# Attention outputs put into their transposed layout by evictions and 32x32 VectorE transposes instead of TensorE transposes

## The chip, the cores and the metric

The kernel runs on one NeuronCore of a Trainium2 chip. TensorE (PE in the profile) multiplies matrices from SBUF into PSUM, whose eight banks each hold 128 partitions x 512 fp32; ScalarE (ACT) and VectorE (DVE) read PSUM and SBUF, GpSimd (POOL) reads and writes SBUF here, and SyncE (SP) issues the DMAs. Each engine executes its own instruction list in order; semaphores tie the lists together. The metric is the device time of one execution in microseconds (us); the kernel before took 704.47 us in the median of three runs (704.37 to 705.89).

## The reference

A transformer block on x of shape (1, 2048, 448) in fp32, with adaLN conditioning:

```python
mod = (_silu(c) @ w_mod).reshape(c.shape[0], 6, 1, -1)     # sa, ca, ga, sb, cb, gb
h = _layernorm(x) * (1 + ca) + sa
x = x + ga * _A_ref(h, A_wqkv, A_wo)       # attention: 16 heads of 28, causal window of 256
h = _layernorm(x) * (1 + cb) + sb
x = x + gb * _B_ref(h, B_w1, B_b1, B_w2)   # 448 -> 1792, mish, 1792 -> 448
```

Attention: for each head, softmax over the keys j with 0 <= i - j < 256 of q.k / sqrt(28), times v; the heads are put side by side and multiplied with wo.

## The kernel before, in words

**Precision.** Nearly every product is made from fp32 values split into a high part (hi, fp32r) and a remainder (lo): x*w is hi*hi + hi*lo + lo*hi, three matmuls. The contraction over 448 rows takes four chunks ci of 128; the last has only 64 rows, and its two halves are used for hi and lo together, so a product takes 3+3+3+2 = 11 matmuls ("passes" and the list `ps` in `gen_wo`).

**Stages.** The 2048 rows are four groups g of 512. After a start of some 48 us, one loop runs over 192 units u: unit u is a third (k = u mod 3) of one head of one group, a slot s = u // 3 being one head. In step u the program emits, in this order: stages of a small pipe (evictions of earlier filler work), `PV(u-3, Pl)`, the eviction `EV` where a head is complete, scores `B(u)` with two exponentials on ACT (P in fp32, Ph in fp32r), `SP(u-1)` (Pl = P - Ph on POOL), a row-maximum pass `A` for a head three slots ahead (a matmul into sA, then a DVE reduction with the mask), every sixth step `M2` (the maxima of two heads turned by TensorE, split on DVE and sent by DMA into rows of q), then filler, and `PV(u-2, Ph)`. A has four tiles a slot: one in each step and a second one at the end of step k = 1. The filler on PE is the QKV projection of the next group and the wo projection of the group before, paid out by a credit (`RATE` us a step). After the loop comes the feed-forward part (two matmul stages, 56 blocks), in which the wo projection of the last group is still interleaved.

**PSUM.** Eight banks: sA 2, sB 2, mm 2 (filler), pv 1, tr 1 (M2's transpose and the output transposes `et`).

**From the head's sum to the wo product.** `PV` accumulates for one head a 60 x 512 tile: rows 0 to 27 from v hi, row 28 the sum of the probabilities (a column of ones in V), rows 32 to 59 from v lo. `EV` (L748) copies it on ACT into half of o2. For two heads together, `E` (L755) turns it by four TensorE transposes into `et`, `E2` (L762) copies the lo part out on ACT, and `E3` (L766) on DVE takes the reciprocal of the sums and adds hi and lo, and on POOL multiplies into `on`, whose rows are tokens. When a group is complete `gen_oT` (L614) turns `on` back by 16 TensorE transposes (`ot`), because the wo matmuls want features on the partitions; ACT takes the high part from PSUM (L624) and DVE the remainder (L619). `gen_wo` (L637) then makes four tiles of 11 matmuls each (issued at L315). `E` and `E3` are emitted once for two heads, 32 times in all; `gen_oT` runs once a group, for the last group in the feed-forward part.

## Time and profile before

| | value |
|---|---|
| median of three runs | 704.47 us (704.37 to 705.89) |
| the profiled execution: span | 703.9 us |
| its own time beside the span | only the span is recorded for it; it lies 0.6 us under the median of the runs |
| start, before the first unit | 0 to 48 us |
| attention loop | 48 to 412 us |
| feed-forward | 412 to 704 us |
| TensorE clock granted | 1.00 in every stage |

Busy shares are shares of the span. A matmul's "mean ns" is its latency from start to modelled end; matmuls overlap, so what one costs in a stream is the distance to the next start, read from the timeline. "Idle before" gives the time an engine stood still before an instruction of a group, and what released it. PEld is the loading of weights, which runs beside PE.

### The profile page before, as it was taken

What the parts mean: (1) busy time and instruction counts of PE and PEld (TensorE: products, weight loads), DVE (VectorE), ACT (ScalarE), POOL (GpSimd) and SP (SyncE); (2) the same over time, 40 slices, a digit from 0 to 9 for tenths busy, and PEclk for the clock granted to TensorE, in tenths of its full rate; (3) what the DMA queues carried; (4) which work ended last, traced back from release to release, by engine and by line L of the source; (5) the groups of instructions that cost most, each with busy time, mean ns of one, the idle gap of its engine ahead of it and who ended that gap; (6) DMA issues with size and microseconds to landing.
All of it is one profiled execution on the core that took longest, in us unless ns stands there. A gap on an engine that the chain in (4) does not pass through costs nothing.

```text
span 703.9 us, 11999 instructions
## 1 busy us (share of the span) xinstructions
PE 685.9 (97%) x4001; PEld 590.2 (84%) x4001; DVE 383.3 (54%) x1030; ACT 391.6 (56%) x740; POOL 326.4 (46%) x355
## 2 busy tenths in 40 slices
PE   9899999999999999999999899999999999999997
PEld 8777888888888888898887788878888888888886
DVE  5688658788655887655768755452224222421112
ACT  3628788777667867667878974344233323332221
POOL 6626779686666776666778957212010000000000
PEclk9999999999999999999999999999999999999999
DMA  7865664455662462663773165800350035001001
GB/s 209 259 221 188 208 204 152 139 181 157 181 209 76 158 207 88 185 211 95 226 216 120 54 203 170 227 20 1 104 117 4 0 106 119 1 1 52 1 1 52
DMA packets 75178, 90.16 MB, mean 128 GB/s; under 512 B 31535, under 2 KB 51741, under 8 KB 75117
## 3 DMA queue, kind: packets, MB, share of 16 engines
q1 hardware_dynamic: 74652, 89.39, 42.0%
q8 instruction: 32, 0.52, 0.3%
q14 instruction: 30, 0.24, 0.1%
q10 hardware_dynamic: 464, 0.00, 0.0%
HBM read 56.60 MB, written 32.51 MB: 127 GB/s over the span
## 4 chain that ended last, share of the span: by engine, by line
PE 78%; DVE 6%; DMA 6%; ACT 3%; POOL 3%; issue 3%; SPq 1%; DVEq 0%; POOLq 0%; ACTq 0%
PE z L917 17%; PE pv L745 10%; PE qk L315 8%; PE sA L683 5%; PE acc L1106 5%; PE acc L1104 5%; PE acc L1105 5%; PE sB L713 5%; PE wo L315 4%; PE qk_v L315 4%; PE sB L724 3%; DMA scr<-st 2%; PE et L759 2%; PE warm L428 1%; DVE junk L685 1%
## 5 line engine op out<-in xcount | busy, mean ns | idle before, releaser
L735 POOL TENSOR_TENSOR Pl<-P,Ph 128x512 fp32r<-128x512 f32 (+2 forms) x192 | 234.8, 1230 | 80.9 <-ACT Ph L728 46.6
L685 DVE CUSTOM_DVE_ANT_0 junk<-sA,mask 128x384 f32<-128x384 f32 (+2 forms) x256 | 135.1, 528 | 95.1 <-PE sA L683 87.4
L727 ACT ACTIVATE P<-sB 128x512 f32<-128x512 f32 (+2 forms) x192 | 109.6, 571 | 62.3 <-PE sB L724 58.1
L925 DVE TENSOR_TENSOR al<-t,ah 128x512 fp32r<-128x512 f32 x56 | 39.2, 700 | 181.8 <-ACT ah L924 181.8
L923 ACT ACTIVATE t<-z,b1c 128x512 f32<-128x512 f32 x56 | 38.3, 684 | 138.6 <-PE z L917 138.6
L728 ACT ACTIVATE Ph<-sB 128x512 fp32r<-128x512 f32 (+2 forms) x192 | 109.2, 569 | 0.0
L683 PE MATMUL sA<-k,q 84*128 84x384 f32 (+2 forms) x256 | 100.5, 396 | 1.8 <-DVE mx L685 1.1
L917 PE MATMUL z<-hlf,w 128*128 128x512 f32 x224 | 88.6, 395 | 0.0
L917 PE MATMUL z<-hhf,w 128*128 128x512 f32 x224 | 88.6, 395 | 0.0
L1104 PE MATMUL acc<-w2h,ah 128*128 128x448 f32 x224 | 82.2, 367 | 1.2 <-ACT ah L924 1.2
L1106 PE MATMUL acc<-w2h,al 128*128 128x448 f32 x224 | 82.1, 366 | 0.1
L1105 PE MATMUL acc<-w2l,ah 128*128 128x448 f32 x224 | 81.6, 364 | 0.0
L745 PE MATMUL pv<-Ph,v 128*60 128x256 f32 (+2 forms) x352 | 76.7, 292 | 0.6 <-ACT o L751 0.5
L745 PE MATMUL pv<-Pl,v 128*60 128x256 f32 (+2 forms) x352 | 74.0, 284 | 2.4 <-POOL Pl L735 1.4
L713 PE MATMUL sB<-q,k 86*128 86x256 f32 (+1 forms) x352 | 74.2, 285 | 0.5 <-DMA q<-mr 0.5
L917 PE MATMUL z<-hhf,w1l 128*128 128x512 f32 x168 | 66.3, 395 | 0.0
L713 PEld LDWEIGHTS sB<-q,k 86*128 86x128 f32 x352 | 61.5, 189 | 2.3 <-DMA q<-mr 1.5
L724 PE MATMUL sB<-fdmask,identr 128*128 128x128 bf16 (+1 forms) x320 | 60.1, 253 | 0.0
L745 PEld LDWEIGHTS pv<-Ph,v 128*60 128x60 f32 x352 | 45.8, 133 | 14.0 <-ACT o L751 1.9
L745 PEld LDWEIGHTS pv<-Pl,v 128*60 128x60 f32 x352 | 45.2, 132 | 11.5 <-POOL Pl L735 3.8
L683 PEld LDWEIGHTS sA<-k,q 84*128 84x128 f32 x256 | 48.9, 193 | 7.0 <-DVE mx L685 4.3
L917 PEld LDWEIGHTS z<-hlf,w 128*128 128x128 f32 x224 | 42.2, 188 | 10.0
(159 smaller groups left out, 1252.4 us busy)
## 6 DMA issues: line engine op xcount, KB each, us to landing
scr<-st SPq DMA_DIRECT2D x24, 512.0 KB
k<-scr SPq DMA_DIRECT2D x48, 252.0 KB
q<-scr SPq DMA_DIRECT2D x64, 168.0 KB
scr<-st SPq DMA_DIRECT2D x32, 256.0 KB
x<-x1d SPq DMA_DIRECT2D x10, 448.0 KB
xin<-in_A_x_dram SPq DMA_DIRECT2D x8, 448.0 KB
xr<-in_A_x_dram SPq DMA_DIRECT2D x16, 224.0 KB
x1d<-xr SPq DMA_DIRECT2D x16, 224.0 KB
```

The costliest lines, as they stand in the source:

```text
L315: PE.matmul(p, b, a, start=(n == 0), stop=(n == 10))
L683: PE.matmul(p[:, c0:384], q[0:84, t * 128:(t + 1) * 128], k[0:84, t * 128 + c0:t * 128 + 384], start=True, stop=True)
L685: DVE.tensor_tensor_reduce(out=junk[:, c0:384], in0=p[:, c0:384], in1=mask[:, c0:384], scale=1.0, scalar=-3.0e38, op0=ALU.add, op1=ALU.max ...
L713: PE.matmul(p[:, c:c + 128 * (t1 - t0)], k[:, jj * 128:(jj + 1) * 128], q[:, t0 * 128:t1 * 128], start=(n == 0), stop=False, skip_group_ch ...
L727: ACT.activation(P[:, c0:], p[:, c0:], AF.Exp, scale=SCALE)
L728: ACT.activation(Ph[u][:, c0:], p[:, c0:], AF.Exp, scale=SCALE)
L735: eng.tensor_tensor(Pl[u][:, a:b], Pt[u][:, a:b], Ph[u][:, a:b].bitcast(F32), op=ALU.subtract)
L745: PE.matmul(pv[0:60, t0 * 128:t1 * 128], V[j % NV][:, h, :], P[u][:, c:c + 128 * (t1 - t0)], start=(P is Ph and b == 0 and n == 0), stop=F ...
L917: PE.matmul(zb[n], ps[m][1], ps[m][0], start=(m == 0), stop=(m == 10))
L1104: PE.matmul(p, ah[n][:, ts], w2h[f], start=(f == 0), stop=False)
L1105: PE.matmul(p, ah[n][:, ts], w2l[f], start=False, stop=False)
L1106: PE.matmul(p, al[n][:, ts], w2h[f], start=False, stop=(f == NF - 1))
```

## The change

In the kernel after, the sums of a head stay with features on partitions. V has 61 columns: lo first (0 to 27), zeros, hi (32 to 59), and the ones column at 60. `on` is one tile of 128 x 4 x 512: chunk ci holds four heads, head j of the four on partitions 32j to 32j+28 (28 features and the sum of probabilities), cleared once at the start. `EV` copies hi and the sum on ACT straight to these partitions. The lo part is added by DVE from PSUM for heads 0 and 1 of the four (`EVlo`), and for heads 2 and 3 is copied by ACT into `tmp` and added by POOL (`add_lo`). Every fourth head, `inverse` turns the chunk in 32x32 blocks on DVE into `tmp`, takes 16 reciprocals a partition, and turns them back, repeated over 32 columns, into `tmp`; `divide` multiplies `on` by `tmp` on POOL. The split into hi (ACT) and lo (DVE) follows from SBUF. wo is laid out in the same padded manner: 32 rows a head, loaded as four pieces of 28 rows a chunk into cleared tiles. So all four chunks are 128 rows and each wo tile takes 12 matmuls instead of 11. `E`, `E2`, `E3` and `gen_oT` are gone; the bank of `tr` goes to pv (2 banks), and `M2` takes one of the two sA banks.

```diff
-    V = [... .tile([128, H, 60], F32R, name=f"v{j}") for j in range(NV)]
+    V = [... .tile([128, H, 61], F32R, name=f"v{j}") for j in range(NV)]
@@ v_out
-            ACT.activation(v[:, :, 0:28], pv, AF.Copy)
+            ACT.activation(v[:, :, 32:60], pv, AF.Copy)
-            DVE.tensor_tensor(v[:, :, 32:60], pv, v[:, :, 0:28].bitcast(F32), op=ALU.subtract)
+            DVE.tensor_tensor(v[:, :, 0:28], pv, v[:, :, 32:60].bitcast(F32), op=ALU.subtract)
@@ wo
-    wol = [mid.tile([128, D], F32R, name=f"wol_{i}", tag="wo", bufs=7) for i in range(3)]
+    wol = [mid.tile([128, D], F32R, name=f"wol_{i}", tag="wo", bufs=8) for i in range(4)]
+    def wo_rows(ci, t):
+        for j in range(4):
+            r = (4 * ci + j) * DH
+            dma(t[32 * j:32 * j + DH], wo[r:r + DH, :])
+            POOL.memset(t, 0.0)
+            later.append(lambda ci=ci, t=t: wo_rows(ci, t))
+    on = mid.tile([128, 4, 512], F32, name="on")
+    POOL.memset(on, 0.0)
@@ in place of gen_oT
+    def split_o(g, ci, pl, own):
+        if ci == 0:
+            OT[g] = new_T(f"o{g}", pl, own)
+        oh, ol = OT[g]
+        ACT.activation(oh[:, ci], on[:, ci], AF.Copy)
+
+        def low():
+            DVE.tensor_tensor(ol[:, ci], on[:, ci], oh[:, ci].bitcast(F32), op=ALU.subtract)
...
+        pipe.add(1, low)
+
+    def split_ready():
+        if ready and (ready[0][0] == 0 or ready[0][0] - 1 in wo_done) and ready[0][0] < NG - 1:
+            split_o(*ready.pop(0), att, "o")
@@ gen_wo
-            for ci in range(3):
+            for ci in range(4):
                 ps += [(oh[:, ci, ts], wo3[ci]), (oh[:, ci, ts], wol[ci]), (ol[:, ci, ts], wo3[ci])]
-            ps += [(oh[:, 3, ts], wo3[3]), (ol[:, 3, ts], wo3[3])]
@@ M2, PV
-        p = bank("tr", 1, f"mt{pr}")
+        p = bank("sA", 2, f"mt{pr}")
+            pvb[i] = bank("pv", 2, f"pv{i}")
@@ in place of EV, E, E2, E3
     def EV(i):
+        g, h = divmod(i, H)
+        ci, j = divmod(h, 4)
+        q = slice(32 * j, 32 * j + DH + 1)
         if i < NS - 3:
+            ACT.activation(on[q, ci], pvb[i][32:61, :], AF.Copy)
+            if j > 1:
+                ACT.activation(tmp[32 * j:32 * j + 32], pvb[i][0:32, :], AF.Copy)
         else:
+            DVE.tensor_copy(on[q, ci], pvb[i][32:61, :])
+    def EVlo(i):
...
+        if j < 2 or i >= NS - 3:
+            o = on[32 * j:32 * j + DH, ci]
+            DVE.tensor_tensor(o, o, pvb[i][0:DH, :], op=ALU.add)
+    def add_lo(n):
...
+            POOL.tensor_tensor(o, o, tmp[64:128], op=ALU.add)
+    def inverse(n):
+        g, ci = divmod(n, 4)
+        DVE.transpose(tmp, on[:, ci])
+        DVE.reciprocal(inv, tmp.rearrange("p (c r) -> p c r", r=32)[:, :, DH:DH + 1])
+        DVE.transpose(tmp.rearrange("p (c r) -> p c r", r=32), inv.to_broadcast([128, 16, 32]))
+    def divide(n):
+        g, ci = divmod(n, 4)
+        POOL.tensor_tensor(on[:, ci], on[:, ci], tmp, op=ALU.mult)
@@ fill_main
-            yield from gen_oT(g - 1, "mm", 2, att, "o")
+            while pipe.held():
+                yield
             yield from gen_qkv(g + 1, (0, 3, 4, 1) + VT)
@@ the loop
+    def outputs(i, u):
+        EV(i)
+        if i % 4 == 3:
+            for d, f in ((1, add_lo), (2, inverse), (3, divide), (5, done_o)):
+                at(u + d, lambda f=f: f(i // 4))
     for u in range(NU + 9):
...
         pipe.step()
+        for f in due.pop(u, ()):
+            f()
+        split_ready()
         if 0 <= u - 3 < NU:
             PV(u - 3, Pl)
             if (u - 3) % 3 == 2:
-                EV((u - 3) // 3)
+                outputs((u - 3) // 3, u)
...
-            if k == 2 and pr >= 0:
-                E(pr)
-        if s % 2 == 0 and k < 2 and 0 <= (s - 4) // 2 < NS // 2:
-            (E2, E3)[k]((s - 4) // 2)
...
         if k == 1 and a < NS:
             A(a, 2)
+        if 0 <= u - 3 < NU and (u - 3) % 3 == 2:
+            EVlo((u - 3) // 3)
```

How the lists move, at three places in the third group (the row says line, operation, output and inputs, shape, and on which engines it waits). First PE, at the end of a slot in which a pair of heads is complete: sA is the maximum pass, et the output transposes, pv the next head's sums. Before:

```order
L683 MATMUL sA_3_3520<-k_0_142,q_0_377 128x384 [waits DVE_49]
L759 MATMUL et_3523<-ident,o_1_465 128x124 x4
L745 MATMUL pv_3531<-Ph_3446,v_171 60x128 [waits Activation_49]
L745 MATMUL pv_3531<-Ph_3446,v_173 60x384
L745 MATMUL pv_3531<-Pl_3487,v_171 60x128 [waits Pool_49]
```

and now:

```order
L693 MATMUL sA_3_3432<-k_0_142,q_0_377 128x384 [waits DVE_49]
L755 MATMUL pv_3439<-Ph_3354,v_171 61x128
L755 MATMUL pv_3439<-Ph_3354,v_173 61x384
L755 MATMUL pv_3439<-Pl_3398,v_171 61x128 [waits Pool_49]
L755 MATMUL pv_3439<-Pl_3398,v_173 61x384
```

The four transposes between the maximum pass and PV are gone, and PV's first matmul no longer waits for ACT. Second DVE, in a step k = 1 (two maximum tiles, ISA junk,mx). Before, the reciprocal and the addition for two heads stand between them:

```order
L685 ISA junk,mx_3451<-sA_0_3547,mask 128x384 [waits PE_49]
L685 ISA mx_3451 128x1
L220 BN_STATS sta_3558<-xin_2838 128x6
L221 BN_AGGR mva_3430<-sta_3558 128x2 [waits DVE_49]
L685 ISA junk,mx_3451<-sA_1_3581,mask 128x384 [waits PE_49]
L685 ISA mx_3451 128x1
L772 RECIPROCAL rc_3584<-et_3523 128x8 [waits Activation_49]
L773 TENSOR_TENSOR ol_3552<-ol_3552,et_3523 128x224 [waits Pool_49]
L685 ISA junk,mx_3451<-sA_2_3599,mask 128x384 [waits DVE_49,PE_49]
L685 ISA mx_3451 128x1
```

and now, in the corresponding place for four heads:

```order
L695 ISA mx_3359 128x1
L703 CAST mr_3365<-mt_3363 8x128 [waits DMAHW5_49,DMAHW4_49,PE_49]
L704 TENSOR_TENSOR mr_3365<-mt_3363,mr_3365 8x128 [waits DVE_49]
L220 BN_STATS sta_3379<-xin_2620 128x6
L221 BN_AGGR mva_3337<-sta_3379 128x2 [waits DVE_49]
L787 STREAM_TRANSPOSE tmp<-on 128x512 [waits Pool_49]
L788 RECIPROCAL inv<-tmp 128x16 [waits DVE_49]
L789 STREAM_TRANSPOSE tmp<-inv 128x512 [waits DVE_49]
L695 ISA junk,mx_3359<-sA_1_3400,mask 128x384 [waits PE_49]
L695 ISA mx_3359 128x1
L695 ISA junk,mx_3359<-sA_2_3411,mask 128x384 [waits DVE_49,PE_49]
L695 ISA mx_3359 128x1
```

The two transposes and the reciprocal stand behind the maximum pass of tile 0 and M2's two small operations, and ahead of the maximum passes of tiles 1 and 2; the first transpose waits for POOL. Third POOL, where Pl is the remainder of the probabilities. Before:

```order
L735 TENSOR_TENSOR Pl_2640<-P_2605,Ph_2606 128x512 [waits PE_49,Activation_49,Pool_49]
L735 TENSOR_TENSOR Pl_2669<-P_2636,Ph_2637 128x512 [waits PE_49,Activation_49,Pool_49]
L775 TENSOR_TENSOR on_2299<-ol_2647,rc_2674 128x4x56 [waits DVE_49]
L735 TENSOR_TENSOR Pl_2704<-P_2665,Ph_2666 128x512 [waits PE_49,Activation_49,Pool_49]
L735 TENSOR_TENSOR Pl_2728<-P_2700,Ph_2701 128x512 [waits PE_49,Activation_49,Pool_49]
L735 TENSOR_TENSOR Pl_2759<-P_2724,Ph_2725 128x512 [waits PE_49,Activation_49,Pool_49]
L735 TENSOR_TENSOR Pl_2791<-P_2755,Ph_2756 128x512 [waits PE_49,Activation_49,Pool_49]
```

and now:

```order
L745 TENSOR_TENSOR Pl_2641<-P_2610,Ph_2611 128x512 [waits PE_49,Activation_49,Pool_49]
L783 TENSOR_TENSOR on<-on,tmp 64x512 [waits Activation_49,Pool_49]
L745 TENSOR_TENSOR Pl_2665<-P_2637,Ph_2638 128x512 [waits PE_49,Activation_49,Pool_49]
L745 TENSOR_TENSOR Pl_2703<-P_2661,Ph_2662 128x512 [waits PE_49,Activation_49]
L793 TENSOR_TENSOR on<-on,tmp 128x512 [waits DVE_49]
L745 TENSOR_TENSOR Pl_2730<-P_2699,Ph_2700 128x512 [waits PE_49,Activation_49]
L745 TENSOR_TENSOR Pl_2755<-P_2726,Ph_2727 128x512 [waits PE_49,Activation_49,Pool_49]
```

One multiplication for two heads has become an addition and a multiplication for four heads; the multiplication waits for DVE and stands ahead of the next Pl.

101 lines of the change are left out of this document (37 added, 64 removed).

## Prediction, made before the result was known

> **What bounds the kernel now.** I read the busy shares first, then a table by stage, then PE's waits, and for each price the timeline. On the profile's page:
>
> ```profile
> PE 685.9 (97%) x4001; PEld 590.2 (84%) x4001; DVE 383.3 (54%) x1030; ACT 391.6 (56%) x740; POOL 326.4 (46%) x355
> ...
> PE 78%; DVE 6%; DMA 6%; ACT 3%; POOL 3%; issue 3%; SPq 1%; DVEq 0%; POOLq 0%; ACTq 0%
> ```
>
> PE fills the span and holds 78% of the chain that ended last. Busy PE is not proof, since a matmul's end is modelled, but the weight loads that run beside it are at 84% too. By stage (time, length, then busy us of PE, PEld, DVE, ACT, POOL, the granted clock, DMA):
>
> ```profile
> 84.00:103.00 19.00, 19.00 (x127) 15.46 (x125) 10.76 (x43) 14.28 (x33) 13.92 (x15) 1.00 0.73 231
> 103.00:122.00 19.00, 19.00 (x128) 16.04 (x127) 15.44 (x47) 16.27 (x39) 17.44 (x17) 1.00 0.46 148
> 122.00:222.00 100.00, 98.73 (x681) 86.64 (x679) 70.76 (x217) 72.47 (x140) 69.01 (x63) 1.00 0.53 164
> 222.00:322.00 100.00, 98.59 (x677) 86.34 (x675) 70.22 (x215) 72.09 (x139) 69.09 (x64) 1.00 0.51 157
> 322.00:369.00 47.00, 46.40 (x318) 39.60 (x318) 31.22 (x98) 35.87 (x71) 34.90 (x30) 1.00 0.65 193
> 369.00:412.00 43.00, 39.36 (x282) 32.81 (x281) 33.06 (x85) 36.17 (x70) 35.35 (x37) 1.00 0.28 86
> 412.00:704.00 292.00, 287.15 (x1334) 248.65 (x1333) 92.84 (x155) 95.98 (x152) 37.50 (x43) 1.00 0.24 69
> ```
>
> The clock is 1.00 throughout. The rows 122 to 322 are groups 1 and 2: PE 98.7 of 100 us, the others near 70. What is taken from PE there comes off the time. In 103 to 122, the end of group 0, POOL has 17.44 of 19 us; in 369 to 412, the loop's end, PE has only 39.4 of 43 and ACT, POOL and DVE stand at 33 to 36: there nothing is gained by PE alone. What PE waits for, in all:
>
> ```profile
> PE pv L745 <- POOL Pl L735: 1.4, 3, 0.5
> ...
> PE sA L683 <- DVE mx L685: 1.1, 3, 0.4
> ```
>
> Both waits are small now, and both are what the change leans on.
>
> **The change part by part: what PE loses and gets.** A stretch of PE's timeline with a pair's four output transposes, then one with four of a group's back transposes, then wo weight loads in a row:
>
> ```profile
> 195.58 0.51 PEld L759 LDWEIGHTS et<-ident,o 124*128 124x128 f32 x4
> ...
> 196.06 0.24 PEld L745 LDWEIGHTS pv<-Ph,v 128*60 128x60 f32 x2
> ...
> 241.86 0.47 PEld L250 LDWEIGHTS ot<-ident,on 128*128 128x128 f32 x4
> ...
> 242.30 0.24 PEld L745 LDWEIGHTS pv<-Ph,v 128*60 128x60 f32 x2
> ...
> 375.14 0.19 PEld L315 LDWEIGHTS wo<-wo,hlo 128*128 128x128 f32 x1
> ...
> 375.35 0.19 PEld L315 LDWEIGHTS wo<-wo,hho 128*128 128x128 f32 x1
> ```
>
> From load to load, four `et` take 196.06 - 195.58 = 0.48 us and four `ot` 242.30 - 241.86 = 0.44; wo matmuls follow at 375.35 - 375.14 = 0.21. So E's 32 quads give 15.4 us, gen_oT's 16 quads 7.0, and 16 more wo matmuls cost 3.4: 19.0 us off PE. By place: group 0 -3.8 (8 quads of et); groups 1, 2 and 3 each -3.8 - 1.8 + 0.8 = -4.8; feed-forward -1.8 + 0.8 = -0.9, the last group's share. PV's matmuls stream the same columns, only 61 instead of 60 weight columns are loaded; the rows below price that.
>
> **What the other engines get.** The rows of the groups on which I draw (name, shapes, count, busy us, mean ns, then idle before):
>
> ```profile
> L1139 DVE STREAM_TRANSPOSE zt<-z 128x512 f32<-128x512 f32 x12 | 8.4, 704 | 0.0
> L339 DVE TENSOR_TENSOR st<-qk,st 128x512 fp32r<-128x512 f32 x28 | 19.2, 686 | 2.5 <-ACT st L336 2.4
> L619 DVE TENSOR_TENSOR hlo<-ot,hho 128x512 fp32r<-128x512 f32 x16 | 10.9, 685 | 5.7 <-ACT hho L624 5.7
> L773 DVE TENSOR_TENSOR ol<-ol,et 128x224 f32<-128x224 f32 x32 | 10.7, 335 | 0.0
> L772 DVE RECIPROCAL rc<-et 128x8 f32<-128x8 f32 x32 | 6.5, 202 | 1.1 <-ACT ol L764 1.1
> L694 DVE TENSOR_TENSOR mr<-mt,mr 8x128 fp32r<-8x128 f32 x32 | 8.9, 279 | 1.1
> L198 DVE TENSOR_TENSOR wol<-wop,wo 128x448 fp32r<-128x448 f32 x3 | 3.5, 1178 | 0.0
> L198 DVE TENSOR_TENSOR w1l<-w1p,w 128x448 fp32r<-128x448 f32 x5 | 3.0, 616 | 0.0
> L220 DVE BATCH_NORM_STATS2 sta<-xin 128x6 f32<-128x448 f32 x16 | 9.9, 618 | 3.6 <-DMA xin<-in_A_x_dram 3.6
> L241 DVE TENSOR_SCALAR xin<-xin,mva,rsa 128x448 f32<-128x448 f32 x12 | 10.1, 840 | 0.5 <-POOL rsa L235 0.5
> L241 DVE TENSOR_SCALAR xn<-x,mv,rsf 128x448 f32<-128x448 f32 x12 | 5.8, 526 | 1.2 <-POOL rsf L235 1.2
> ...
> L735 POOL TENSOR_TENSOR Pl<-P,Ph 128x512 fp32r<-128x512 f32 x155 | 201.9, 1307 | 73.5 <-ACT Ph L728 40.8 <-PE sA L683 11.4 <-POOL Pl L735 6.4
> L775 POOL TENSOR_TENSOR on<-ol,rc 128x224 f32<-128x224 f32 x32 | 18.3, 573 | 21.7 <-DVE ol L773 9.1 <-ACT Ph L728 8.9 <-PE ot L250 1.5
> L160 POOL MEMSET mask<- 128x384 f32 x1 | 0.4, 422 | 0.1
> ...
> L751 ACT ACTIVATE o<-pv 60x512 f32<-60x512 f32 x61 | 35.9, 589 | 22.7 <-PE pv L745 22.3
> L764 ACT ACTIVATE ol<-et 128x224 f32<-128x224 f32 x32 | 11.7, 366 | 0.0
> ...
> L713 PEld LDWEIGHTS sB<-q,k 86*128 86x128 f32 x352 | 61.5, 189 | 2.3 <-DMA q<-mr 1.5
> L745 PEld LDWEIGHTS pv<-Ph,v 128*60 128x60 f32 x352 | 45.8, 133 | 14.0 <-ACT o L751 1.9 <-issue 0.6
> ```
>
> Weights: 128 columns load in 189 ns, 60 in 133, so a column is 0.8 ns; 704 loads get at most 0.6 us, hidden where a load lies beside a matmul. I take nothing.
>
> DVE, for four heads. Gone are two reciprocals and two additions, 2 x (0.20 + 0.34) = 1.07 us. New: two EVlo, a PSUM and an SBUF operand on 512 columns like L339, 1.37; two transposes and a reciprocal, the `inverse`, 0.70 + 0.20 + 0.70 = 1.6. DVE rises by 1.9 us in about 25, from 71 to 78%. The 0.70 is from the feed-forward, where POOL is idle. Beside a running POOL (the loop) three sorts of DVE work are to be seen: a pass with two SBUF inputs takes 1178 ns instead of 616 (L198), L241's scaling of one input 840 instead of 526, and L220 with one input stays at 618. The transpose has one input and the pace of L220 (512/704 = 448/618 = 0.73 elements a ns; L241 alone makes 448/526 = 0.85), so 0.70 is my value; the bounds are 0.70 and 0.70 + 0.56.
>
> The Trainium skill says the same of the cause: "SBUF — State Buffer", section "Who interferes with whom", has a VectorE instruction with at most one SBUF input outside the two-port modes free of contention with GpSimd, and one with two SBUF inputs contending with GpSimd's reads. By that rule the transposes are free, which the trace cannot show before they run beside POOL, and it speaks against another part of the change: the remainder of the split read PSUM and SBUF, and now reads SBUF twice.
>
> That remainder (L619, 685 ns) is priced by L198: 0.56 us more, 16 times, 9 us of DVE, none of it on a chain that PE waits for directly, since a group's wo is due much later. I take nothing, and keep 0 to 4 us for the range.
>
> What decides is the place of `inverse`. It stands behind M2's two DVE passes (0.55 us with L693's copy) and ahead of the step's two maximum passes. How far PE runs ahead of DVE there:
>
> ```profile
> 193.31 0.42 PE L683 MATMUL sA<-k,q 84*128 84x384 f32 x1
> 193.76 0.56 DVE L685 CUSTOM_DVE_ANT_0 junk<-sA,mask 128x384 f32<-128x384 f32 x1 [1.08 <-PE sA L683]
> ...
> 194.87 0.56 DVE L685 CUSTOM_DVE_ANT_0 junk<-sA,mask 128x384 f32<-128x384 f32 x1 [0.54 <-PE sA L683]
> ...
> 195.47 0.42 PE L683 MATMUL sA<-k,q 84*128 84x384 f32 x1
> ```
>
> The pass of 193.76 has freed its bank at 194.32 and PE takes it again at 195.47: 1.15 us of slack, and DVE stood idle 0.54 us before the next pass. A block of 1.6 us uses up the idle time (0.54) and nearly all the slack (1.06 of 1.15), and costs PE nothing when DVE comes to it early. With M2's 0.55 and another eviction (0.69) still in front it is late by up to 1.2. M2 now also turns up in sA's two banks, which shortens the distance between two uses of a bank. Bounds 0 and 1.2, I take 0.45 us for each of the 15 blocks of the loop, 1.8 a group.
>
> POOL, for four heads: 2 x 0.57 goes, an addition (64 partitions, the same 512 columns) and a multiplication of 1.31 each come: +1.5 us. In groups 1 and 2 POOL goes from 69 to 75% and this is hidden; but `divide` waits for DVE with the next Pl behind it, and PV waits for that Pl. In group 0 POOL is short: its last quarter gets 17.44 + 1.5 = 18.9 us of work for 19 us, and clearing the four wo tiles adds 4 x 0.45 = 1.8 (an estimate from L160's 422 ns for 384 columns). So group 0's 3.8 us are eaten by 1.8 of blocks and 2.5 of POOL: +0.5. Clearing `on`, some 2 us by the same row, falls into POOL's idle time before the loop:
>
> ```profile
> 40.38 0.23 POOL L234 TENSOR_SCALAR rsa<-mva 128x4 f32<-128x4 f32 x1 [8.41 <-DVE mva L221]
> ```
>
> ACT: EV stays, E2's 2 x 0.37 goes and two copies of 0.59 come: +0.45 us in 25, hidden. DMA: eleven more issues for wo on SP, three slots ahead of anything due; nothing.
>
> Group 3: its first half is PE's (46.4 of 47): two times four heads, -2.9 with the wo tiles, +0.9 for two blocks, -2.0. Its second half (369 to 412) gets 1.5 us more POOL and 1.9 more DVE twice with no idle engine to take them, and the filler that ends sooner leaves only steps that ACT and POOL set; I put +2.0 there, so 0 for the group.
>
> **The sum.** Group 0 +0.5, groups 1 and 2 each -4.8 + 1.8 = -3.0, group 3 0, feed-forward -0.9: -6.4 us on the span of 703.9 gives 697.5. The median of the runs is 0.6 above that span, so 698.1.
>
> **The rivals.** (a) All of PE's 19.0 us arrive: 703.9 - 19.0 + 0.6 = 685.5. For it: PE's waits on DVE and POOL are small in the table above. Against it: the stages 84 to 122 and 369 to 412.
>
> (b) Slower: the DVE block holds sA. If each transpose loses 0.56 to POOL, the block is 2.7 us, late by 0.45 + 1.12 = 1.6, and with `divide` then late too, the next Pl comes late: by its row POOL idles 73.5/155 = 0.47 us ahead of a Pl, so `divide`'s 1.31 makes it 0.84 late, of which I let half, 0.4, reach PE. 15 x 2.0 = 30 against 19.0 gives 703.9 + 11 + 0.6 = 715.5. It decides from 19.0/15 = 1.27 us of stall a block; below that the change gains. For it speaks the order of the rows on DVE, with three passes in one piece and in front of both banks' readers; against it the single input.
>
> (c) No change: a stall of about 1.27 us a block, the gain and the blocks cancel, 704.
>
> That the transposes stay in the program some other way is excluded by the instruction lists.
>
> **How the numbers follow.** A gain in part, 690 to 703, is likeliest with 0.57 (prediction 698); all or nearly all of it, below 690, has 0.15; cancelled 0.10; slower 0.18. Two runs are told apart from about 0.2%, 1.4 us. Faster by more is 0.57 + 0.15 = 0.72, the same 0.10, slower 0.18. The range 689 to 708 leaves out some 0.12 below and 0.10 above.
>
> **What would show it.** PE's busy time falls by about 18 us and the 192 transposes of `et` and `ot` are gone; DVE rises by about 30; groups 1 and 2 take some 97 us each instead of 100. `inverse` shows transposes of 0.70 us; PE's wait for sA on DVE grows from 1.1 to about 7 us, and that for Pl by 2 to 4, at the start and end of the loop. The prediction is wrong if the transposes take over 1.2 us, if sA's wait passes 19 us, or if groups 1 and 2 keep their 100 us with PE idle; and, the other way, if group 0 gets shorter by its full 3.8.

## The result, and the profile after

The changed kernel takes 727.57 us in the median of four runs (725.52 to 728.81), the kernel before, on the same chip, 705.18 (704.37 to 706.62): a ratio of 1.031 (95% interval 1.029 to 1.034). 698 was forecast, and 708 was the upper end of the range. The change makes the kernel slower by 22 us. (A few single executions of kernels below were disturbed and took 950 to 1670 us; they are left out, and the one profile that fell on such an execution, e1's, isn't read.)

The page of the changed kernel, engines and chain:

```profile
PE 684.1 (94%) x3825; PEld 580.0 (80%) x3825; DVE 423.1 (58%) x1048; ACT 405.0 (56%) x738; POOL 353.8 (49%) x353
...
PE 67%; DVE 12%; ACT 5%; issue 4%; DMA 4%; POOL 1%; SPq 1%; DVEq 0%; POOLq 0%; ACTq 0%
```

PE has 176 matmuls fewer (4001 to 3825), yet its busy time falls by only 1.8 us, and its part of the chain falls from 78% to 67% while DVE's goes from 6% to 12%. Next the time by stage. The borders are the first score matmul of each group, the middle of group 3, and the first matmul of the feed-forward's second product (the first product starts 6 us before it, at 406.7 and 421.2 us, among the last heads); columns are as in the prediction's table. Before:

```profile
122.00:221.60 99.60, 98.33 (x676) 86.29 (x675) 70.36 (x217) 72.17 (x140) 69.01 (x63) 1.00 0.53 164
221.60:321.80 100.20, 98.81 (x679) 86.50 (x678) 70.50 (x215) 72.38 (x140) 69.01 (x63) 1.00 0.51 157
321.80:369.00 47.20, 46.57 (x318) 39.80 (x319) 31.33 (x99) 35.87 (x71) 34.98 (x30) 1.00 0.65 193
369.00:413.20 44.20, 40.56 (x288) 33.57 (x287) 34.20 (x87) 37.10 (x72) 35.35 (x37) 1.00 0.30 92
```

and the change:

```profile
124.50:226.80 102.30, 97.42 (x632) 83.45 (x632) 79.55 (x219) 75.80 (x140) 74.84 (x62) 0.98 0.52 158
226.80:327.80 101.00, 96.20 (x634) 82.53 (x634) 79.37 (x219) 75.66 (x140) 74.81 (x62) 1.00 0.52 157
327.80:377.60 49.80, 45.62 (x299) 38.53 (x299) 36.14 (x103) 37.65 (x71) 39.54 (x29) 1.00 0.69 207
377.60:427.20 49.60, 42.67 (x259) 35.11 (x260) 37.12 (x84) 37.89 (x69) 37.62 (x35) 0.86 0.21 65
427.20:449.70 22.50, 16.28 (x65) 12.99 (x64) 12.81 (x17) 10.03 (x19) 14.37 (x12) 0.92 0.60 188
```

Groups 1 and 2 take 102.3 and 101.0 us where they took 99.6 and 100.2, and PE is now idle for 5 us in each. The two halves of group 3 grow from 47.2 to 49.8 and from 44.2 to 49.6. The granted clock, 1.00 in every stage before, is 0.98, 0.86 and 0.92 in three of these rows. What PE waited for (us in all, times, longest):

```profile
PE sA L693 <- DVE mx L695: 8.2, 14, 1.7
PE pv L755 <- POOL Pl L745: 6.6, 10, 2.5
PE wo L315 <- DVE hlo L624: 4.5, 1, 4.5
PE sB L723 <- DMA q<-mr: 3.3, 1, 3.3
PE tr L250 <- DVE xin L241: 3.2, 2, 1.6
```

Against before these five have grown by 7.1, 5.2, 4.5, 2.8 and 3.2 us: 22.8 together. A sum over the distances between PE's matmul starts closes the account. What a matmul needs at full clock is estimated as its columns at 2.21 a ns, for a transpose at 1.17 (the medians of the distances before), or the distance to the next start where that is shorter; what a stretch at half clock adds to it is its price, and the rest is waiting. The need falls by 13.2 us, the stretches at half clock cost 9.6, and the waits grow by 25.3: 21.7 of the 21.9 by which the span grew.

Were the new operations priced rightly? Groups of DVE and POOL in the changed kernel:

```profile
L777 DVE TENSOR_TENSOR on<-on,pv 28x512 f32<-28x512 f32 x34 | 22.8, 671 | 0.6
L787 DVE STREAM_TRANSPOSE tmp<-on 128x512 f32<-128x512 f32 x16 | 11.1, 695 | 0.0
L789 DVE STREAM_TRANSPOSE tmp<-inv 128x512 f32<-128x512 f32 x16 | 11.4, 712 | 0.6
L624 DVE TENSOR_TENSOR hlo<-on,hho 128x512 fp32r<-128x512 f32 x16 | 17.4, 1099 | 2.1 <-ACT hho L621 2.1
L783 POOL TENSOR_TENSOR on<-on,tmp 64x512 f32<-64x512 f32 x15 | 19.2, 1283 | 9.0 <-ACT tmp L768 8.0 <-PE pv L755 0.6
L793 POOL TENSOR_TENSOR on<-on,tmp 128x512 f32<-128x512 f32 x16 | 21.0, 1311 | 15.9 <-DVE tmp L789 15.6
```

The transposes take 695 and 712 ns beside a running POOL, as forecast (0.70). The remainder of the split takes 1099 ns instead of 685, +0.41 where +0.56 was the price. The Trainium skill, "SBUF — State Buffer", section "Who interferes with whom", has one SBUF input free of GpSimd and two contending with its reads; these rows agree in both.

**One block and what follows it.** DVE's timeline in the second half of group 3 (start, length, line, operation):

```profile
385.80 0.28 DVE L704 TENSOR_TENSOR mr<-mt,mr 8x128 fp32r<-8x128 f32 x1
386.01 1.30 DVE L198 TENSOR_TENSOR w1l<-w1p,w 128x448 fp32r<-128x448 f32 x1
387.23 0.70 DVE L787 STREAM_TRANSPOSE tmp<-on 128x512 f32<-128x512 f32 x1
387.96 0.25 DVE L788 RECIPROCAL inv<-tmp 128x16 f32<-128x16 f32 x1
388.25 0.71 DVE L789 STREAM_TRANSPOSE tmp<-inv 128x512 f32<-128x512 f32 x1
388.88 0.52 DVE L695 CUSTOM_DVE_ANT_0 junk<-sA,mask 128x384 f32<-128x384 f32 x1
```

and the changed kernel's stretches around it (the clock is the column after POOL's):

```profile
384.00:388.00 4.00, 3.29 (x23) 2.19 (x21) 3.75 (x11) 3.95 (x9) 3.65 (x4) 1.00 0.16 61
388.00:392.00 4.00, 2.53 (x11) 2.14 (x12) 3.82 (x10) 1.85 (x5) 4.00 (x4) 0.62 0.77 204
392.00:396.00 4.00, 4.00 (x20) 3.24 (x18) 3.94 (x9) 2.64 (x5) 4.00 (x6) 0.53 0.04 12
```

M2's second pass, a split of a weight tile (1.30, not in the forecast's picture) and `inverse` stand in one piece from 385.8 to 388.9, and the maximum pass behind them begins only then. This is the 1.7 us wait in the row of sA. From 388.9 on the clock is 0.50 for 6.8 us (the rows are means over 4 us), and PE, with work again, does it at half speed: beside its stall of 1.7 us the block costs up to 3.4 more, half of that stretch.

**The start of the feed-forward part.** First a row of POOL's waits in the changed kernel, then DVE's timeline:

```profile
POOL on L793 <- DVE tmp L789: 15.6, 8, 7.9
```

```profile
428.95 0.68 DVE L777 TENSOR_TENSOR on<-on,pv 28x512 f32<-28x512 f32 x1
430.28 0.70 DVE L787 STREAM_TRANSPOSE tmp<-on 128x512 f32<-128x512 f32 x1
431.31 0.71 DVE L789 STREAM_TRANSPOSE tmp<-inv 128x512 f32<-128x512 f32 x1
434.62 2.27 DVE L624 TENSOR_TENSOR hlo<-on,hho 128x512 fp32r<-128x512 f32 x2 [2.10 <-ACT hho L621]
441.82 2.21 DVE L624 TENSOR_TENSOR hlo<-on,hho 128x512 fp32r<-128x512 f32 x2
```

The last head's sum is complete with the addition of 428.95, but what follows is a chain: POOL waits 7.9 us for the inverse, ACT's and DVE's split of the last chunk follows from 434 to 444, and PE, whose filler reaches the wo tile after four steps (`gen_oT` had eight there), stands 4.5 us on hlo with nothing else to do.

### The profile page after: what moved, and what is told of

Its sections match the earlier page's. It is cut to its first block, busy times and chain, and to the rows that moved or that the text cites. A ratio compares the mean times of both kernels' runs of the same rounds, so it can differ in the third digit from the quotient of the medians.

```text
span 725.8 us, 11759 instructions
## 1 busy us (share of the span) xinstructions
PE 684.1 (94%) x3825; PEld 580.0 (80%) x3825; DVE 423.1 (58%) x1048; ACT 405.0 (56%) x738; POOL 353.8 (49%) x353
## 4 chain that ended last, share of the span: by engine, by line
PE 67%; DVE 12%; ACT 5%; issue 4%; DMA 4%; POOL 1%; SPq 1%; DVEq 0%; POOLq 0%; ACTq 0%
PE z L935 17%; PE pv L755 8%; PE qk L315 7%; PE acc L1136 5%; PE acc L1134 5%; PE acc L1135 5%; PE sA L693 5%; PE wo L315 4%; PE sB L723 4%; DVE junk L695 3%; PE qk_v L315 3%; PE sB L734 3%; DMA scr<-st 2%; POOL Pl L745 1%; ACT P L737 1%
## 5 line engine op out<-in xcount | busy, mean ns | idle before, releaser
L693 PE MATMUL sA<-k,q 84*128 84x384 f32 (+2 forms) x256 | 102.5, 404 | 9.2 <-DVE mx L695 8.2
L755 PE MATMUL pv<-Pl,v 128*61 128x256 f32 (+2 forms) x352 | 75.8, 290 | 6.7 <-POOL Pl L745 6.6
L723 PE MATMUL sB<-q,k 86*128 86x256 f32 (+1 forms) x352 | 76.3, 291 | 4.3 <-DMA q<-mr 3.3
L755 PE MATMUL pv<-Ph,v 128*61 128x256 f32 (+2 forms) x352 | 77.3, 294 | 0.0
L723 PEld LDWEIGHTS sB<-q,k 86*128 86x128 f32 x352 | 63.3, 195 | 7.5 <-issue 4.1
L693 PEld LDWEIGHTS sA<-k,q 84*128 84x128 f32 x256 | 49.8, 195 | 18.4 <-DVE mx L695 13.9
L755 PEld LDWEIGHTS pv<-Pl,v 128*61 128x61 f32 x352 | 45.9, 136 | 17.1 <-POOL Pl L745 10.2
L755 PEld LDWEIGHTS pv<-Ph,v 128*61 128x61 f32 x352 | 48.0, 138 | 13.2 <-issue 0.9
L224 POOL COPY xn<-xn 128x64 f32<-128x64 f32 x12 | 5.0, 429 | 98.2 <-DVE xn L241 98.2
```

Source lines behind the costliest of these rows:

```text
L693: PE.matmul(p[:, c0:384], q[0:84, t * 128:(t + 1) * 128], k[0:84, t * 128 + c0:t * 128 + 384], start=True, stop=True)
L723: PE.matmul(p[:, c:c + 128 * (t1 - t0)], k[:, jj * 128:(jj + 1) * 128], q[:, t0 * 128:t1 * 128], start=(n == 0), stop=False, skip_group_ch ...
L755: PE.matmul(pv[0:61, t0 * 128:t1 * 128], V[j % NV][:, h, :], P[u][:, c:c + 128 * (t1 - t0)], start=(P is Ph and b == 0 and n == 0), stop=F ...
```

## The experiments

Sixteen kernels were run beside the kernel before and the change; two further runs, d2 and d3, repeat c1. All are built on the changed kernel unless the text says otherwise. The letters in the expectations are theories: P, the filler's pace (steps that went with `gen_oT` lay waits open); D, VectorE's block and load hold the scores' banks; O, POOL's additions and divisions delay Pl; C, waits and clock set the time and TensorE's work does not; M, the maxima's turn in sA's banks. R, S, F, U and G are explained where they stand. Half clock is the length of the stretches at a granted clock of 0.50 in the profiled execution; the other columns are PE's waits there, in us.

| kernel | median us | ratio to before (95%) | sA on DVE | Pl on POOL | hlo | xin | half clock |
|---|---|---|---|---|---|---|---|
| before | 705.2 | 1 | 1.1 | 1.4 | 0 | 0 | 0 |
| the change | 727.6 | 1.031 (1.029 to 1.034) | 8.2 | 6.6 | 4.5 | 3.2 | 20.5 |
| e1_pace | 731.4 | 1.037 (1.034 to 1.040) | | | | | |
| e2_ff | 723.9 | 1.027 (1.024 to 1.031) | 8.1 | 7.5 | 1.1 | 3.2 | 13.7 |
| e3_both | 725.6 | 1.030 (1.028 to 1.031) | 8.0 | 7.9 | 1.1 | 0 | 27.3 |
| e4_late | 735.2 | 1.043 (1.042 to 1.045) | 12.2 | 10.4 | 1.1 | 0 | 41.0 |
| n1_noinv | 720.6 | 1.023 (1.019 to 1.027) | 3.9 | 8.6 | 4.7 | 3.1 | 13.7 |
| n2_nopool | 723.7 | 1.026 (1.024 to 1.029) | 10.9 | 2.4 | 4.7 | 3.2 | 13.7 |
| n3_dummy | 737.6 | 1.046 (1.044 to 1.048) | 9.7 | 5.1 | 4.5 | 3.2 | 23.9 |
| n4_m2bank | 789.8 | 1.119 (1.116 to 1.122) | 5.0 | 1.5 | 4.5 | 3.2 | 61.4 |
| b1_bare | 710.9 | 1.008 (1.004 to 1.012) | 5.0 | 2.2 | 3.7 | 4.0 | 3.4 |
| b2_nodve | 717.4 | 1.016 (1.011 to 1.021) | 2.9 | 7.7 | 4.7 | 3.1 | 20.5 |
| b3_actlo | 722.6 | 1.027 (1.023 to 1.031) | 7.3 | 7.2 | 4.5 | 3.1 | 17.1 |
| b4_best | 721.0 | 1.022 (1.021 to 1.024) | 7.3 | 7.2 | 1.1 | 3.1 | 17.1 |
| c1_barepace | 705.2 | 1.000 (0.998 to 1.003) | 2.4 | 4.4 | 1.1 | 0 | 0 |
| c2_bareff | 712.0 | 1.008 (1.006 to 1.010) | 5.0 | 2.4 | 1.1 | 4.1 | 10.2 |
| c3_block | 715.1 | 1.014 (1.012 to 1.015) | 6.9 | 1.3 | 0 | 0 | 0 |
| d1_all | 720.4 | 1.021 (1.018 to 1.024) | 7.3 | 7.0 | 1.1 | 0 | 17.1 |

**First: pace against block, by mending them.** e1 puts four empty filler steps where the four turns of the stack had stood, e2 makes the last split give two steps a piece, e3 does both, and e4 does both and besides cuts the block in two (`inverse` is there the first turn with the reciprocal, `turn_back` the second turn) and puts each half at a step's end, behind the maximum passes.

```diff
@@ e1, fill_main
             while g - 1 not in on_split:
                 yield
+            for _ in range(4):
+                yield
@@ e2, gen_split
             split_o(g, ci, FW["ff"], "")
             yield
+            yield
@@ e4, for all but the last four heads (those one step earlier than in the change); add_lo stays, done_o comes one step later
-            for d, f in ((1, add_lo), (2, inverse), (3, divide), (5, done_o)):
+                at_end(u + 2, lambda: inverse(n))
+                at_end(u + 4, lambda: turn_back(n))
+                at(u + 5, lambda: divide(n))
```

> The kernel after, with four empty filler steps put ahead of the wo projection, where the back transposes stood before. Theory P (pace: the filler now comes to work whose data is late, and the stalls also lower the granted clock): the gaps ahead of the transposes of xin (1.8 us at 154.8 and 257.3) and the wait of 3.5 us for the maxima at 373.9 go, with the stretches of half clock at 157 and 379 (2 x 1.7 us): 727.6 falls by 8 to 11 us, to 717 to 720. Theory D (the VectorE block of transposes ahead of the maximum passes is what costs the time): under 3 us, as the next wait takes over.

> The kernel after, with the split of the last group's outputs spread over eight instead of four steps of the feed-forward part. Theory P: the wait of the wo matmul for hlo at 438.6 (4.7 us) and the stretch of half clock after it (1.7 us) go: 5 to 7 us less, 721 to 722.5. Theory D: at most 2 us, since the chain from the last block of transposes through GpSimd to the split ends as late as before.

> Both edits of pace together. Theory P: the two add up, 13 to 18 us less, 709.5 to 714.5, with at most two stretches of half clock left. Theory D: 723 or more.

> Both edits of pace, and the VectorE block cut in two and put behind the maximum passes: the first transpose at the end of the step, reciprocal and second transpose at the end of the step after next, the division one step behind that; the last chunk's block stands earlier in the loop's end. Theory P: 2 to 3 us under the kernel with both edits alone. Theory D: TensorE's wait for sA on VectorE falls from 8 us to 2, the stalls at 387.5 and 411.8 and their half clock (10 us of it) go: 8 to 12 us under it. Both theories together make 700 to 706.

Only e2 came near its number: 723.9, and hlo falls from 4.5 to 1.1 us as meant. e1 is 731.4, e3 725.6, and e4, of which D expected nearly all, is 735.2, the slowest of the four. In e3 the waits that were aimed at are gone from the table (hlo 1.1, xin 0), and the time isn't: half clock grew from 20.5 to 27.3 us. In e4 it is 41.0 (6.8 of it in the start, before the first unit), and sA's wait 12.2. P's numbers fail in e1, e3 and e4; D's hold for e3 (723 or more) and fail in e4, where D expected the most. So moving stalls about doesn't end them, and both theories in this form fell.

**Second: parts left out, one at a time.**

```diff
@@ n1: tmp is filled with ones once
-            for d, f in ((1, add_lo), (2, inverse), (3, divide), (5, done_o)):
+            for d, f in ((1, add_lo), (3, divide), (5, done_o)):
@@ n2
+            for d, f in ((2, inverse), (5, done_o)):
@@ n3, PV, first of each two heads
+                for t in range(4):
+                    PE.transpose(pvb[i][:, t * 128:(t + 1) * 128], ident, ident)
@@ n4: banks as before the change
-        p = bank("sA", 2, f"mt{pr}")
+        p = bank("tr", 1, f"mt{pr}")
-            pvb[i] = bank("pv", 2, f"pv{i}")
+            pvb[i] = bank("pv", 1, f"pv{i}")
```

> The kernel after without the two transposes and the reciprocals (left out: the outputs are not divided by the sums; the GpSimd multiplication stays and reads a tile of ones, and no longer waits for VectorE). Theory D (the VectorE block holds the maximum passes): TensorE's wait for sA falls from 8 us to about 2, the wait for Pl at 411.8 goes, at most two stretches of half clock: 12 to 18 us under the kernel after, 710 to 715. Theory O (GpSimd's two operations ahead of Pl): at most 4 us under it.

> The kernel after without GpSimd's addition of the low part and without its multiplication (left out: low part of two heads in four, and the division; VectorE's block stays). Theory O: the waits for Pl (6.6 us) go and half of the half clock, 8 to 12 us under the kernel after. Theory D: at most 4 us.

> The kernel after with the work that the change took from TensorE put back as empty work: four transposes of the identity for two heads, 32 x 0.48 = 15.4 us, into the bank of pv before its sums start. If TensorE's work still sets the pace: 15 us slower. Theory C (TensorE waits for others and loses clock in these waits): 0 to 6 us slower, or faster, with fewer than five stretches of half clock.

> The kernel after with PSUM shared out as before: a bank of its own for the turned maxima, one bank for pv. Theory M (the maxima in sA's two banks shorten the reuse of a bank): the waits for sA fall by half, 5 us faster or more. If the second bank of pv is worth more, since the low part is read from it by VectorE at the end of a step: slower by 5 us or more. Theory D alone: within 3 us.

Without the turns the kernel is 7 us faster (720.6), without POOL's two operations 4 (723.7); each takes down its own wait (sA 8.2 to 3.9; Pl 6.6 to 2.4) and lets the other grow (Pl to 8.6; sA to 10.9). Neither part is the cause by itself: n1 falls between D's and O's numbers, and n2, with half of what O expected, stays at D's bound. n3, between its two numbers, says that TensorE's work still sets much of the pace: 32 quads of transposes that nobody needs cost 10 us, 0.31 a quad. n4 shows why the change gave the bank to pv. With one bank PE waits, in its table,

```profile
PE pv L755 <- DVE on L777: 50.3, 31, 3.1
```

for `EVlo`, which reads the head's bank on DVE behind the step's maximum passes. sA's wait falls from 8.2 to 5.0 in it. Since n4 gives M2 its own bank and takes one from pv at once, what M is worth by itself isn't shown.

**Third: everything left out.** b1 drops `EVlo`, the copy into tmp, `add_lo`, `inverse` and `divide` at once. b2 is n1 without `EVlo` for the first two heads of four, so that DVE's busy time is 383.8 us against 383.3 before the change. b3 moves the lo rows of all four heads to ACT and POOL; b4 is b3 with e2's edit and the last inverse a step earlier.

```diff
@@ b1 (and `if False` for EVlo and the copy)
-            for d, f in ((1, add_lo), (2, inverse), (3, divide), (5, done_o)):
+            for d, f in ((5, done_o),):
@@ b2, EVlo
-        if j < 2 or i >= NS - 3:
+        if i >= NS - 3:
@@ b3
-            if j > 1:
-                ACT.activation(tmp[32 * j:32 * j + 32], pvb[i][0:32, :], AF.Copy)
+            if 0 < j and i < NS - 4:
+                lo_copy(i)
-            o = on[64:128, ci]
-            POOL.tensor_tensor(o, o, tmp[64:128], op=ALU.add)
+            o = on[:, ci]
+            POOL.tensor_tensor(o, o, tmp, op=ALU.add)
```

> The changed kernel with all of its new work left out: no addition of the lower rows, no copy into tmp, no sum, no transposes, no reciprocals, no division; EV writes the unnormalized product alone, and the split and the padded wo stay. PE does the changed kernel's matmuls (12.4 us less work than before). Theory R (TensorE's saving is real and only what was added beside it eats it): 704.5 - 12.4 and nothing else, 690 to 696, no stretch at half clock in the middle of the groups. Theory S (the skeleton itself eats it: fewer filler steps, the split that reads two SBUF tiles, the later start of the feed-forward, the half clock behind each stall): 708 to 720.

> As the run without the transposes and reciprocals, and besides the addition of the lower rows into SBUF (the 671 ns one) left out for the first two heads of each four, so that these heads lack half of their product; tmp is filled with ones once, GpSimd's sum and division stay. DVE is then some 11 us under the run without the transposes, near its load before. Theory D (it is VectorE's load that holds TensorE): 704 to 711, TensorE's wait on the scores' tile 2 us or less. Theory R (GpSimd's sum and division, or the path, hold it and VectorE's load no more): 718 to 723.

> The changed kernel, but the lower rows of all four heads go the way of the last two: ScalarE copies them into tmp (the first head's two steps later) and GpSimd adds them on 128 partitions at once; the last four heads stay with VectorE. VectorE loses 30 instructions of 0.67 us, 20 us; ScalarE gains 30 of 0.59, 18 us; GpSimd's instructions stay 15 in number. Theory D: 715 to 721 (6 to 12 us under the change), TensorE's wait on the scores' tile from 8 to 3 us. Theory R (no single engine, the path ends at the same places): 725 to 730, since what VectorE gives ScalarE takes.

> The run before it with two more edits: the split gives a step of filler back per piece (as in the run that paced the feed-forward's start) and the last four heads' transposes and division come one step earlier. Theory D with the late start of the feed-forward as the second cause: 710 to 717, TensorE's 4.7 us wait on hlo gone. If the half clock sets in at other stalls instead (as with the two paced edits together): 722 to 728. Under 704 from neither.

b1 is the run that turned the study. With none of the new work on DVE, ACT or POOL but the split from SBUF, and all of TensorE's savings, the kernel takes 710.9 us: still not under the kernel before. Its page and PE's waits in it:

```profile
PE 672.1 (95%) x3825; PEld 573.8 (81%) x3825; DVE 380.9 (54%) x966; ACT 388.2 (55%) x708; POOL 312.8 (44%) x322
PE sA L693 <- DVE mx L695: 5.0, 9, 1.0
PE tr L250 <- DVE xin L241: 4.0, 2, 2.0
PE wo L315 <- DVE hlo L624: 3.7, 1, 3.7
```

PE's busy time is down by 13.8 us (685.9 to 672.1), and by the account above the need by 14.3 (635.5 to 621.2); the waits grew by as much (63.1 to 77.2), and its one stretch at half clock cost 1.7. Theory S holds: 17 of the 22 us come with the added work (727.6 - 710.9), and the other 6, and the whole of TensorE's saving besides, are lost by the frame without it. b2 lies between D's and R's numbers, 717.4: DVE's load is a part, and POOL's, still in, keeps Pl's wait at 7.7. b3 and b4 take 5 and 6.6 us off the change; 722.6 and 721.0 lie between the numbers of their two theories.

**Fourth: where the bare kernel loses TensorE's saving, and the block alone.** c1 is b1 with both edits of pace (e1's and e2's), c2 with e2's alone. c3 is the kernel before with a block of VectorE work at the points where the change has `inverse`:

```diff
@@ c3, on the kernel before
+    def block():
+        for _ in range(3):
+            DVE.transpose(junk, mask)
@@ the loop
         pipe.step()
+        if u % 12 == 4 and u > 4:
+            block()
```

> The run with all of the change's new work left out, and on it both edits of pace: four empty filler steps where the four turns of the stack stood, ahead of each group's wo tiles, and two filler steps for each piece of the last split. Theory F (TensorE's saving went into waits that the lost filler steps laid open: xin 4.0 us, hlo 3.7, scores' tile 5.0): the span of 706.0 falls by 4 + 3.7 and part of the 5, to 696 to 700; TensorE's waits on xin and hlo under 1 us each. Theory U (the units' own loop, from scores over maxima and exponentials to P times V, and not the filler, sets the groups' time): 702 to 708; those two waits may go, but as much comes up at other places.

> The run with all of the change's new work left out, and on it the last split's two filler steps for each piece alone. Theory F: 3.5 to 4 us under the run without it, a span of 702, the wait on hlo gone and the groups as they were. Theory U: the feed-forward's start costs as much with other work in the gap: 705 to 707.

> The kernel before, with three VectorE transposes of the mask into the scratch tile of the max passes (about 0.5 us each) at 16 places, each at the point in the program where the change puts its turn, reciprocal and turn back: 1.6 us of VectorE in one block, with nothing that waits for its result. The block alone, as the prediction priced it (0.45 us of stall each at 15 places): 0.3 to 0.5 us a block, 709 to 713. If VectorE has the slack where TensorE is full: 704 to 706. If each stall also brings a stretch at half clock: 715 or more.

c1 is 705.2, nearly 6 us under b1: the lost filler steps cost that much, and the two edits that took 2 us off the full change (e3) do more here. Yet it only equals the kernel before. xin's wait is gone and sA's is 2.4, but in their place

```profile
PE pv L756 <- POOL Pl L746: 4.4, 7, 1.2
PE sB L724 <- DMA q<-mr: 2.7, 4, 1.5
```

which were 1.4 and 0.5 before. In c1's profiled execution PE's matmuls need 13.6 us less, and waits take 9.8 of it. Its span, 700.6, is just above F's numbers, its median inside U's. By stage (table below) F is right for groups 1 and 2, which gain 5.5 us, and U for the rest: group 0 and group 3 gain 1.9 together, and the feed-forward part is 4.1 longer. c2's hlo is mended like e2's, but its 712.0 is above both theories' numbers and no gain on b1's 710.9, with 10.2 us of half clock in its profile against 3.4.

c3 takes 715.1, 9.8 us over the kernel before, at a clock of 1.00. Its block and its wait:

```profile
L678 DVE STREAM_TRANSPOSE junk<-mask 128x384 f32<-128x384 f32 x48 | 27.4, 571 | 1.1
PE sA L687 <- DVE mx L689: 6.9, 13, 1.3
```

48 transposes at 571 ns are 1.71 us a block; 9.8 us over 16 blocks is 0.61 each. sA's wait grew by 5.8 of the 9.8, the rest is small waits. The block that the forecast priced at 0.45 us costs 0.61 in a kernel whose filler is as it was: more than the 709 to 713 expected, and not by the clock.

**Fifth: the clock, and everything together.** d1 is b4 with e1's four steps. d2 and d3 are c1 again, unaltered.

> A version that computes the same as the change: the lower rows of all heads by ScalarE and GpSimd, the last four heads' inverse a step earlier, two filler steps for each piece of the last split, and the four empty filler steps ahead of each group's wo tiles. Theory F (the pace is worth what it was worth in the kernel without the added work, 6 to 7 us): 713 to 716. Theory G (stalls that the added work makes close the clock gate wherever they fall, and the pace moves them and does not end them): 719 to 726, with 3 or more stretches at half clock. Neither gives less than 704.

> The kernel with all of the change's new work left out and both edits of pace, once more: its ten executions lay between 701.9 and 709.7, where those of the kernel before lay within 2.7 us. Theory G (in some executions a stall falls so that the clock gate closes for a stretch of 3.4 us or more): an execution over 705 shows one or more stretches at a granted clock of 0.5, one near 702 none. If the clock stays at 1.00 in an execution over 705, the spread has another cause.

> The same kernel a third time, for the same comparison: a profile of a longer or of a shorter execution. Theory G: the time above 702 is about half of the half-clock stretches' length, 1.7 us for each 3.4; otherwise no such relation.

d1 is 720.4 and no better than b4 (721.0): the four steps were worth 6.8 us in the bare kernel (c2 to c1) and are worth 0.6 here. That is G's range, with four stretches at half clock. It is the best version with the change's result, and 2.1% slower than the kernel before; since c1, with none of the new work but the split, only reaches the kernel before, nothing here beats it.

c1, d2 and d3 show when half clock sets in. Three profiles of one kernel: spans of 700.6 us with no stretch at half clock, 701.0 with one (3.4 us), 703.7 with two (6.8). In each execution all changes of the granted clock lie on a grid of 3.413 us, whose place differs from one execution to the next. The same place of the program by the windows of that grid (borders to 0.1 us), first in c1, then the two windows in d2, then two in d3:

```profile
347.60:351.00 3.40, 1.86 (x16) 1.45 (x15) 0.58 (x4) 1.60 (x3) 2.11 (x2) 1.00 0.93 227
```

```profile
345.60:349.00 3.40, 2.69 (x19) 2.12 (x17) 1.48 (x6) 2.43 (x5) 2.06 (x3) 1.00 0.91 279
349.00:352.40 3.40, 1.91 (x13) 1.78 (x14) 1.04 (x3) 1.09 (x2) 0.94 (x1) 1.00 0.92 211
```

```profile
347.00:350.40 3.40, 1.36 (x11) 0.96 (x9) 0.57 (x3) 1.59 (x3) 2.10 (x2) 1.00 0.90 241
350.40:353.80 3.40, 3.33 (x12) 2.98 (x13) 1.64 (x4) 1.09 (x2) 0.90 (x1) 0.50 0.90 204
```

In d2 and d3 PE is idle 2.2 and 2.1 us at 348, for the same reason (scores waiting for the maxima's DMA). In d2 the clock stays at 1.00; in d3 it falls to 0.50 for 3.4 us, and the twelve units from 350.5 on take 23.7 us instead of 22.2. The grid is what differs: in d2 a border cuts the gap, and PE is idle for 0.7 us of one window and 1.5 of the next; in d3 nearly the whole gap, 2.0 us, lies in one window, and the next runs at half clock. Two stalls between 423 and 428 (0.8 and 1.1 us, for the split at the start of wo) leave PE idle for 1.55 us of one window in c1, 1.62 in d2 and 1.71 in d3: no stretch in c1, one in d2 and d3. Half the length, 1.7 us a stretch, isn't met exactly (d2 is 0.4 us over c1, d3 2.7 over d2), since the waits differ a little too. In times, c1's profiled execution took 702.4 us without a stretch, d2 702.8 with one, d3 705.5 with two: the order is G's, but d2 has a stretch near 702, where G expected none.

## Why the prediction was wrong, step by step

The forecast was 6.4 us less on the span, and it grew by 21.9. Three steps failed above all. PE's saving was mis-sized, 14.2 us and not 19.0. Group 3 and the feed-forward part, put at 0 and -0.9, grew by 8.0 and 7.9: the sum had no term for the filler steps that went with `gen_oT`, and nothing for the split (hlo), on which PE waited 4.5 us. And the clock was taken as 1.00, where half clock cost 9.6.

By stage, in us of change against the span of 703.9 (profiled executions; the borders are the same points of the program in each trace):

| stage | forecast | the change | b1 (bare) | c1 (bare, paced) |
|---|---|---|---|---|
| start and group 0 | +0.5 | +2.5 | +1.3 | -0.5 |
| group 1 | -3.0 | +2.7 | -1.6 | -2.5 |
| group 2 | -3.0 | +0.8 | -1.8 | -3.0 |
| group 3 | 0 | +8.0 | -1.5 | -1.4 |
| feed-forward | -0.9 | +7.9 | +5.7 | +4.1 |
| sum | -6.4 | +21.9 | +2.1 | -3.3 |

- **PE's saving, -19.0 us.** Mis-sized. By the distances between the starts of the matmuls in the profile before, the 128 `et` took 11.3 us and not 15.4 (0.35 a quad), the 64 `ot` 6.1 and not 7.0; the 16 more wo matmuls cost 3.2. That is 14.2 us, and b1, without the added work, shows 13.8 less busy time. The distance from the quad's first weight load to the next load behind it, 0.48, was not what the quad kept from the others: PE begins what follows 35 ns after the last transpose's start on the average, where the others of a quad are 105 apart.
- **What bounds the kernel: PE, 98.7 of 100 us in groups 1 and 2, so "what is taken from PE there comes off the time".** With the corrected size a group there has 3.5 us less PE work. With the pace given back 2.5 and 3.0 of it arrive (c1), without it 1.6 and 1.8 (b1). Upward it holds too (n3: 32 quads more, 10 us). This step stands, for groups 1 and 2 and a kernel in which nothing else is changed. Elsewhere the prediction's own table had said that PE's time isn't the limit, and c1 gains 0.5 in group 0 and 1.4 in group 3.
- **The weight column, nothing.** Loads took 136 to 138 ns instead of 132 to 133; agreed.
- **DVE's prices.** Transposes 0.70: right (695, 712). The reciprocal 0.25 us instead of 0.20, EVlo 671 ns for 686, the remainder 1099 for 685 + 560. DVE's busy time rose by 39.8, not 30; 6.6 of it is the remainder, which the prediction had priced at 9 and left out of its 30.
- **The `inverse` block, 0.45 us at 15 places.** Alone in the kernel before it is 0.61 (c3), inside the bounds of 0 to 1.2. In the change the turns are worth 7 us (n1), about 0.47 a block, though some of that is clock (half clock 20.5 to 13.7). The mechanism held, and the size was of the right order. What was missed is that such a stall can be paid a second time in the clock.
- **POOL, hidden in groups 1 and 2.** In these groups (124.5 to 327.8 us) PE's wait for Pl is 1.5 us, so this nearly holds there; elsewhere it fell, with Pl 1.4 to 6.6 in all, and 2.5 us of it in one piece at 412, behind a `divide` that waits for DVE. `divide` and the sum are worth 4 us (n2).
- **Group 3, 0, and feed-forward, -0.9.** The largest miss, 16.8 of 28.3 us. The prediction had only counted PE's work at the feed-forward's start and not the chain from the last head through inverse, divide and split to wo, nor that the filler there went from eight steps to four. It called DMA nothing; a 3.3 us wait of scores on the maxima's DMA at 374, with the DMA engines at 0.93 of their time, was new:

```profile
372.00:376.00 4.00, 2.24 (x17) 1.67 (x14) 1.96 (x8) 2.94 (x6) 2.29 (x3) 1.00 0.93 283
```

- **Filler steps.** The prediction treated `gen_oT`'s turns as PE time alone. They were also steps of the filler, four in each of three groups and eight at the end (four now), behind which xin was normalized and hlo split. Giving them back is worth nearly 6 us without the new work (b1 to c1).
- **The clock, "1.00 throughout".** It was read in the profile before and taken as given for the profile after. 20.5 us at half clock cost 9.6.
- **Rival (b)** had the right sign and the right first place, but its mechanism (transposes slowed by POOL, 1.27 us of stall a block) did not happen. What happened was no block over 1.27 us on average: the sum of waits at five places, the clock, and a smaller gain.
- **"What would show it".** PE's busy time fell by 1.8 rather than 18; groups 1 and 2 kept, and passed, their 100 us with PE idle, which the prediction had named as proof against it; sA's wait came to 8.2 (7 forecast), Pl's rise to 5.2 (2 to 4).

What stays open: how much of the 17 us of the added work goes to the clock can't be told by leaving work out, since each such edit moves the stalls. For the two profiled executions, b1's and the change's, the account above gives 7.9 us to half clock (9.6 against 1.7) and 11.2 to waits (25.3 against 14.1). Of the 4.1 us by which the feed-forward part is longer in c1, four waits that the kernel before has not make 3.0 (hlo 1.1, its high part on ACT 0.8, and 0.8 and 0.3 elsewhere); the rest was not traced.

## What to carry to other kernels

Before building what replaces an expensive operation, leave the operation out with nothing in its place: b1 and c1 would have told ahead of all the rest that taking TensorE's transposes away is worth some 3 us in the best profiled execution here, and nothing in the median. An instruction that goes from a schedule counted in steps takes its step with it, and whatever that step was hiding. And work moved from the engine that is full to those at 70% is not free where they stand in one loop with it: short stalls of the matrix engine can cost twice, once in idle time and once in the clock.
